# Splitting a weight load and a copy at the start of a fused attention and gated-MLP kernel, and reordering the last additions at its end

## The chip, the cores and the metric

The kernel runs on one core of a Trainium2 chip. The metric is device time in microseconds (us), taken over several executions of the same program. Every execution also leaves the span of the core (first to last instruction), which is about 1.7 us shorter than its time. One execution of each kernel is profiled in full.

All profile lines below are in microseconds from the start of the span unless marked ns. PE is TensorE, PEld its weight loads, DVE is VectorE, ACT is ScalarE, POOL is GpSimd, SP is SyncE; a name with q (SPq, ACTq) is an engine's instruction that issues a DMA.

## The reference, cut to what matters

```python
xn  = layernorm(x)                      # x: 2048 tokens x 512
A   = sliding_window_attention(xn @ wqkv) @ wo      # 32 heads of 16, 8 keys, dilation 2
B   = (z1 * (w_sp @ layernorm(z2) + b_sp)) @ w_out   # z1, z2 = gelu(xn @ w_in), a gated MLP
out = x + A + B
```

Two places matter here. At the start nothing can be multiplied before the first tokens are loaded, normalised and transposed, and before the q weights (a 512 x 512 part of `wqkv`) are there. At the end the last 512 tokens are accumulated in PSUM, `x` is added, and the sum is stored.

## The kernel before: the parts that matter

Tokens are handled in tiles of 128. The first block `t0` has four tiles, each normalised by VectorE, transposed by TensorE into PSUM (`tr`) and copied out by ScalarE (`tr_copy`). TensorE is kept busy at the start by matmuls on a tile of zeros (`warm_up`), which are meant to have its clock full earlier: in this document's profiles it was full by 6.93 us in eleven of the twelve with ten or more of these matmuls (9.82 in the other), and only from 10.21 and 9.50 us in the two with one.

```python
load_x0(SP, 0, 0, 64)           # first token tile, two halves on two queues
load_x0(A, 0, 64, P)
load_x0(A, 1)                   # second token tile
G.dma_start(xall[:, 0, 2:4, :], xblk[0][:, 2:4, :])
load_wqk(SP, 0)                 # q weights, 512 KB
SP.dma_start(xall[:, 1], xblk[1])
load_wqk(SP, 1)                 # k weights, 512 KB
# [cut]
def tr_copy(i, pt):
    A.copy(xnT[:, :, i * P:(i + 1) * P], pt[:])
# [cut]
warm_up(10)
for n in range(2):
    ln_stats(t0[n]); ln_sqrt(col(t0[n]))
for n in range(2):
    ln_tile(t0[n])
    tr_copy(t0[n], tr(t0[n]))
warm_up(1); warm_up(1, 2)
for n in range(2, 4):
    ln_stats(t0[n]); ln_sqrt(col(t0[n]))
for n in range(2, 4):
    ln_tile(t0[n])
pqs = [qk_tile() for _ in range(3)]
qk_part(pqs[0], 0, 0, 0, 2)     # the first q matmuls: eight of 256 columns
tr_copy(t0[2], tr(t0[2]))       # third token tile
```

At the end, the last group's four token tiles (`tb`) lie in PSUM tiles `po` (tb 0 and 1 share one), `pa` (tb 2, and columns 0 to 287 of tb 3) and `pb` (the other 224 columns of tb 3). The order list ends with `Oh3.0 s2.1 Oh3.1 F3.0 F3.1 s3.0 s3.1`: matmuls of tb 0 and 1, matmuls of tb 2 and 3, then `F` (the additions of tb 0 and 1) and `s` (their stores).

```python
def out_half(o, h):
    if o == 3 and h == 1:
        for tb, part, E in ((2, 0, SP), (3, 0, A), (3, 1, SP)):
            out_full(o, tb, part)       # matmuls
            out_add(o, tb, part)        # VectorE: PSUM + x
            out_store(o, tb, part, E)
    else:
        for tb in (2 * h, 2 * h + 1):
            out_full(o, tb)
```

So in VectorE's program the additions of tb 2 and 3 stand before those of tb 0 and 1, although TensorE finishes in the order 0, 1, 2, 3.

## Time and profile before

| | before |
|---|---|
| time, median of the first 3 runs | 206.78 us (206.6 to 207.16) |
| span of the profiled run | 206.2 us |
| first q matmul starts | 8.10 us |
| last matmuls of the last group (po) start | 197.40 us |
| last addition ends | 203.30 us |

The page of the profile, busy time per engine and the chain that ended last (shares of the span):

```profile
PE 199.2 (97%) x1695; PEld 126.2 (61%) x1699; DVE 180.8 (88%) x259; ACT 97.3 (47%) x159; POOL 5.6 (3%) x15
...
PE 94%; DMA 2%; DVE 1%; issue 1%; DVEq 0%; ACTq 0%
```

What TensorE waited for in the whole run (the waits view: total, times, longest):

```profile
PE pwm L547 <- DVE warm L183: 1.1, 1, 1.1
PE pt L221 <- DVE r_x L214: 0.8, 1, 0.8
PE po L520 <- issue: 0.6, 4, 0.2
```

TensorE is the limit from the first q matmul to the end of the last group; a change can gain only before and after that. This is the tail in the timeline (start, duration, engine, line, operation, tiles, count, and in brackets the idle time before it and what ended it):

```profile
199.34 1.85 PE L520 MATMUL pa<-r_w,r_uz 128*128 128x512 bf16 x10
200.62 1.07 DVE L510 TENSOR_TENSOR r_qk<-pa,r_qk 128x512 bf16<-128x512 f32 x2 [6.10 <-PE pa L520]
201.71 0.39 DVE L510 TENSOR_TENSOR r_qk<-pb,r_qk 128x224 bf16<-128x224 f32 x1
202.02 1.28 DVE L510 TENSOR_TENSOR r_qk<-po,r_qk 128x512 bf16<-128x512 f32 x2
```

The additions of `po` come last, at 202.02, though the matmuls that fill `po` had ended before 199.6; VectorE had been idle for 6.10 us before it began with `pa`. And this is the head, the same view:

```profile
1.06 4.45 PE L547 MATMUL pwm<-warm 128*128 128x512 bf16 x10 [1.06 <-DVE warm L183]
6.30 1.13 PE L221 MATMUL pt<-ident,r_x 128*128 128x128 bf16 x8 [0.79 <-DVE r_x L214]
6.94 1.11 ACT L225 COPY xnT<-pt 128x512 bf16<-128x512 bf16 x2 [0.87 <-PE pt L221]
7.22 0.84 PE L547 MATMUL pwm<-warm 128*128 128x512 bf16 x2
8.10 1.86 PE L306 MATMUL pq<-xnT,r_w 128*128 128x256 bf16 x8
```

The two transposed tiles are copied from 6.94 to 8.05, and the first q matmul follows at 8.10. The eight q matmuls take 1.86 us, starting 0.21 to 0.22 us apart, so TensorE still runs at half clock here: in the same trace 32 of them, from 10.84 us on, take 3.49 us by the chain of waits, 0.109 us each.

### The profile page before, as it was taken

Reading aid. Unit: us, or ns where it says so; the run is one execution under the profiler, and the core shown is the slowest. Engines: PE = TensorE matmul, PEld = TensorE weight load, DVE = VectorE, ACT = ScalarE, POOL = GpSimd, SP = SyncE. Lnnn points to the kernel's source line nnn. Section 1 sums busy time; section 2 is a strip of 40 time slices with the busy share of each in tenths; the row PEclk is TensorE's granted clock in tenths of the full one; section 3 lists DMA queues with packets and bytes.
Section 4 is the critical chain, followed back from the end, with each engine's and each line's share of the span. In section 5 each row is a group of like instructions: output and inputs, shape, how many; then the busy total and the mean of one; then the engine's idle time right before and its main releaser. Section 6 shows DMA issues by size and latency. Waiting matters only on the chain.

```text
span 206.2 us, 4083 instructions
## 1 busy us (share of the span) xinstructions
PE 199.2 (97%) x1695; PEld 126.2 (61%) x1699; DVE 180.8 (88%) x259; ACT 97.3 (47%) x159; POOL 5.6 (3%) x15
## 2 busy tenths in 40 slices
PE   7899999999999999999999999999999999999991
PEld 2598866555566666666566666664566654664650
DVE  3979799899679999969999999999999998589604
ACT  3375998879899787634303755430032230020000
POOL 5000000500000000000000000000000000000000
PEclk9999999999999999999999999999999999999998
DMA  5972547400000693199960599998389000465523
GB/s 137 356 257 53 102 101 239 107 0 0 3 0 3 155 182 73 38 234 224 157 168 21 114 199 181 253 206 188 89 152 235 10 3 0 115 147 167 155 97 103
DMA packets 65826, 25.91 MB, mean 126 GB/s; under 512 B 56208, under 2 KB 65488, under 8 KB 65552
## 3 DMA queue, kind: packets, MB, share of 16 engines
q1 hardware_dynamic: 65360, 25.12, 54.9%
q0 software_dynamic: 80, 0.26, 0.5%
q10 hardware_dynamic: 368, 0.27, 0.5%
q8 instruction: 13, 0.21, 0.5%
q14 instruction: 5, 0.04, 0.1%
HBM read 10.13 MB, written 2.10 MB: 59 GB/s over the span
## 4 chain that ended last, share of the span: by engine, by line
PE 94%; DMA 2%; DVE 1%; issue 1%; DVEq 0%; ACTq 0%
PE pg L448 36%; PE pz L235 18%; PE pq L306 14%; PE po L520 7%; PE pv L409 7%; PE po L496 6%; PE pl L359 2%; DMA r_x<-in_A_x_dram 2%; PE pt L221 1%; PE pa L520 1%; PE po L505 1%; PE pb L496 1%; DVE r_qk L510 1%; PE pa L306 0%; DVEq L687 0%
## 5 line engine op out<-in xcount | busy, mean ns | idle before, releaser
L448 PE MATMUL pg<-z,r_qk 128*128 128x344 bf16 x448 | 67.0, 309 | 0.0
L448 PEld LDWEIGHTS <-r_qk 128*128 128x128 bf16 x448 | 43.8, 98 | 21.8
L235 PE MATMUL pz<-w_z,xnT 128*128 128x344 bf16 x256 | 40.3, 309 | 0.0
L423 DVE TENSOR_TENSOR r_pr<-r_x,r_w 128x2048 bf16<-128x2048 bf16 x32 | 38.2, 1218 | 0.4
L454 ACT ACTIVATE gs<-pg,b_col 128x688 bf16<-128x688 f32 x16 | 13.2, 831 | 53.7 <-PE pg L448 53.6
L427 DVE TENSOR_TENSOR r_pr<-r_pr 128x2048 bf16<-128x2048 bf16 x28 | 33.9, 1216 | 0.1
L235 PEld LDWEIGHTS <-xnT 128*128 128x128 bf16 x256 | 24.8, 98 | 13.8 <-issue 1.2
L340 DVE TENSOR_TENSOR r_pr<-r_qk 128x2048 bf16<-128x2048 bf16 x24 | 28.2, 1218 | 2.5 <-ACT r_qk L316 2.5
L306 PE MATMUL pq<-xnT,r_w 128*128 128x256 bf16 (+1 forms) x176 | 29.7, 323 | 0.0
L306 PEld LDWEIGHTS <-r_w 128*128 128x128 bf16 x184 | 20.5, 115 | 7.5 <-issue 0.6
L316 ACT CAST r_qk<-pq 128x1024 bf16<-128x1024 f32 (+1 forms) x16 | 15.4, 993 | 3.7 <-PE pq L306 3.4
L297 ACT ACTIVATE r_uz<-pz 128x688 bf16<-128x688 f32 x16 | 11.6, 744 | 9.7 <-PE pz L235 9.5
L520 PE MATMUL po<-r_w,r_uz 128*128 128x512 bf16 x66 | 14.9, 379 | 0.6 <-issue 0.6
L409 PE MATMUL pv<-xnT,r_w 128*32 128x512 bf16 x256 | 14.6, 380 | 0.0
L496 PE MATMUL po<-r_lg,r_pr 32*128 32x512 bf16 x224 | 14.5, 375 | 0.0
L520 PEld LDWEIGHTS <-r_uz 128*128 128x128 bf16 x85 | 8.0, 98 | 9.8 <-issue 1.5
L351 DVE TENSOR_TENSOR r_pr<-r_pr 128x4096 bf16<-128x4096 bf16 x6 | 13.5, 2285 | 0.0
L203 DVE BATCH_NORM_STATS2 stats<-r_x 128x6 f32<-128x512 bf16 x16 | 10.8, 673 | 2.1 <-DMA r_x<-in_A_x_dram 2.1
L259 ACT ACTIVATE junk<-z 128x688 bf16<-128x688 bf16 x16 | 12.5, 781 | 0.1
L409 PEld LDWEIGHTS <-r_w 128*32 128x32 bf16 x256 | 9.5, 138 | 4.5 <-issue 0.3
L253 ACT ACTIVATE z<-pz 128x688 bf16<-128x688 f32 x16 | 11.8, 741 | 0.5 <-PE pz L235 0.5
L496 PEld LDWEIGHTS <-r_pr 32*128 32x128 bf16 x272 | 7.6, 93 | 6.5 <-issue 0.9
(80 smaller groups left out, 164.0 us busy)
## 6 DMA issues: line engine op xcount, KB each, us to landing
r_lg<-in_A_wo_dram SPq DMA_DIRECT2D x8, 256.0 KB, 4.1
r_qk<-in_A_x_dram SPq DMA_DIRECT2D x16, 128.0 KB, 2.4
out_dram<-r_qk SPq DMA_DIRECT2D x15, 128.0 KB, 2.1
r_w<-in_A_wqkv_dram SPq DMA_DIRECT2D x3, 512.0 KB, 5.6
r_x<-in_A_x_dram SPq DMA_DIRECT2D x3, 512.0 KB, 6.2
w_z<-in_B_w_in_dram SPq DMA_DIRECT2D x2, 688.0 KB, 6.7
r_w<-in_B_w_out_dram SPq DMA_DIRECT2D x1, 640.0 KB, 5.1
r_x<-in_A_x_dram POOLq DMA_DIRECT2D x1, 256.0 KB, 4.3
```

Of the source, the lines that this page charges most:

```text
L235: PE.matmul(pz[:, hh, 0:FHALF], xnT[:, kc, i * P:(i + 1) * P], wz[:, kc, hh * FHALF:(hh + 1) * FHALF], start=(kc == 0), stop=(kc == C - 1))
L306: PE.matmul(pq[:, cc, p0 * P:(p0 + b1 - b0) * P], wqk[:, sd, kc, c0 + cc:D:C], xv[:, kc, b0:b1, j, :], start=(kc == 0), stop=(kc == C - 1))
L316: cast = A.copy(dst, pq[:, :, p0 * P:(p0 + b1 - b0) * P].rearrange("p c (b t) -> p c b t", b=b1 - b0))
L340: prod = V.tensor_tensor(pr[g % 3][:, c].rearrange("p w b t -> p b w t"), q3.unsqueeze(2).broadcast_to([P, TB, 4, P]), k4, ALU.mult)
L351: V.tensor_tensor(pr[g % 3][:, 0:2], pr[g % 3][:, 0:2], pr[g % 3][:, 2:4], ALU.add)
L409: PE.matmul(pv[32 * tb:32 * tb + 32, dd, :], wv[:, kc, 2 * d2 + dd, :], xnT[:, kc, tb * TBS:(tb + 1) * TBS], start=(kc == 0), stop=(kc == ...
L423: V.tensor_tensor(pw_t[n], vp[:, :, off:off + P], a_sb[:, slot_w(w), ts].unsqueeze(1).broadcast_to([P, DH, P]), ALU.mult)
L427: V.tensor_tensor(pw_t[n] if dst is None else dst, pw_t[n], pw_t[m], ALU.add)
L448: PE.matmul(pg[:, hh, 0:FHALF], wsp[n][:, k, :], z2[:, k, hh * FHALF:(hh + 1) * FHALF], start=(k == 0), stop=(k == NT - 1))
L454: A.activation(gs[:], tiles.pop(("g", n))[:, :, 0:FHALF], ACT.Identity, bias=b_col[:, i:i + 1])
L496: PE.matmul(pc, op[32 * tb:32 * tb + 32, d, o * P:(o + 1) * P], wo_r[32 * tb:32 * tb + 32, d, cs], start=(d == 8), stop=False, tile_positi ...
L520: PE.matmul(pc, uT[:, o % 2, m, tb * P:(tb + 1) * P], wout[:, m, cs], start=False, stop=(m == MCH - 3))
```

## The change

Four edits: the q weights come as two halves (rows 0 to 255 and 256 to 511) over the queues of SyncE and ScalarE; the second token tile is copied in two halves, and the first q matmuls are ordered so that those that need only the first half come first; one more warm-up matmul fills the wait before the transposes; and the last group's additions are issued in the order in which TensorE completes them. (The diff also generalises two helpers that give the same program as before; cut here.)

```diff
-Oh3.0 s2.1 Oh3.1 F3.0 F3.1 s3.0 s3.1
+Oh3.0 s2.1 Oh3.1 F3.0 F3.1 s3.0 s3.1 end
# [cut]
-    load_wqk(SP, 0)
+    load_wqk(SP, 0, 0, 2)
+    load_wqk(A, 0, 2, 4)
# [cut]
-    def tr_copy(i, pt):
-        A.copy(xnT[:, :, i * P:(i + 1) * P], pt[:])
+    def tr_copy(i, pt, c0=0, c1=C):
+        A.copy(xnT[:, c0:c1, i * P:(i + 1) * P], pt[:, c0:c1, :])
# [cut: qk_part gets kcs, the row quarters to multiply]
     def out_half(o, h):
-        if o == 3 and h == 1:
-            for tb, part, E in ((2, 0, SP), (3, 0, A), (3, 1, SP)):
+        for tb in (2 * h, 2 * h + 1):
+            for part in range(len(tiles["o", o][tb])):
                 out_full(o, tb, part)
-                out_add(o, tb, part)
-                out_store(o, tb, part, E)
-        else:
-            for tb in (2 * h, 2 * h + 1):
-                out_full(o, tb)
+
+    def last_adds():
+        for tb, part, E in ((2, 0, SP), (3, 0, A), (3, 1, SP)):
+            out_add(3, tb, part)
+            out_store(3, tb, part, E)
# [cut]
-    warm_up(10)
+    warm_up(11)
# [cut]
-        tr_copy(t0[n], tr(t0[n]))
+    tr_copy(t0[0], tr(t0[0]))
+    pt1 = tr(t0[1])
+    tr_copy(t0[1], pt1, 0, 2)
+    tr_copy(t0[1], pt1, 2, 4)
# [cut]
-    qk_part(pqs[0], 0, 0, 0, 2)
+    qk_part(pqs[0], 0, 0, 0, 2, kcs=range(2))
+    qk_part(pqs[0], 0, 0, 0, 2, kcs=range(2, 4))
```

More of the change, by code (lines that the diff above doesn't have):

```diff
@@ L40 @@
 ORD = [1, 2, 3, 0]
-PAIRED = (0, 1, 2, 3, 4, 5, 6, 7)
+CHUNKS = (2, 2, 2, 2, 2, 2, 2, 2)
 ORDER = """
@@ L165, in load_x0, with load_wqk @@
         E.dma_start(xall[p0:p1, 0, tb, :], x2[tb * TBS + p0:tb * TBS + p1, :])
-    def load_wqk(E, s):
-        E.dma_start(wqk[:, s],
-                    A_wqkv[:, s * D:(s + 1) * D].rearrange("(k p) f -> p k f", p=P))
+    def load_wqk(E, s, k0=0, k1=C):
+        E.dma_start(wqk[:, s, k0:k1],
+                    A_wqkv[:, s * D:(s + 1) * D].rearrange("(k p) f -> p k f", p=P)[:, k0:k1])
     load_x0(SP, 0, 0, 64)
@@ L298, in z1_gelu, with qk_part @@
                      tiles.pop(("x", n))[:, :, 0:FHALF], ACT.Gelu_apprx_tanh)
-    def qk_part(pq, j, m, b0, b1, ccs=(0, 1), p0=None):
+    def qk_part(pq, j, m, b0, b1, ccs=(0, 1), p0=None, kcs=range(C)):
         sd, c0 = m // 2, 2 * (m % 2)
@@ L304, in qk_part @@
         for cc in ccs:
-            for kc in range(C):
+            for kc in kcs:
                 PE.matmul(pq[:, cc, p0 * P:(p0 + b1 - b0) * P], wqk[:, sd, kc, c0 + cc:D:C],
@@ L348, in pair_add, with pair_add2 @@
     def pair_add(g):
-        if g not in PAIRED:
-            return
         V.tensor_tensor(pr[g % 3][:, 0:2], pr[g % 3][:, 0:2], pr[g % 3][:, 2:4], ALU.add)
+    def pair_add2(g):
+        V.tensor_tensor(pr[g % 3][:, 0], pr[g % 3][:, 0], pr[g % 3][:, 1], ALU.add)
     def logits(g):
@@ L355, in logits @@
         pl = ps_aux.tile([P, 4, P], F32, name="pl", tag="aux")
-        n_c = 2 if g in PAIRED else C
+        n_c = CHUNKS[g]
         for c in range(n_c):
@@ L650 @@
     st = z2_var(3, 3) + [z2_log, z2_exp]
-    steps = {"z": z2_mm, "zg": z2_gelu, "zs": z2_sq, "q": qk_mm, "qc": qk_cast, "p": prod_c, "a": pair_add,
+    steps = {"z": z2_mm, "zg": z2_gelu, "zs": z2_sq, "q": qk_mm, "qc": qk_cast, "p": prod_c, "a": pair_add, "b": pair_add2,
              "L": logits, "Lc": logits_cast, "V": v_mm, "Vc": v_cast, "X": z1_mm, "Xg": z1_gelu,
@@ L656 @@
              "G": g_mm, "Gi": g_bias, "U": u_mul, "T": u_tr, "A": lambda k: ap[k](),
-             "O": out_heads, "Or": out_rest, "Oh": out_half, "F": out_add, "s": out_store,
+             "O": out_heads, "Or": out_rest, "Oh": out_half, "F": out_add, "s": out_store, "end": last_adds,
              "halo": halo_zero, "wo": load_wo, "late": load_late, "xr": load_xr, "w": load_wsp}
```

## The prediction

> **What bounds the kernel.** TensorE: the page gives PE 97% of the 206.2 us span, the chain of waits is 94% PE. Between 8.1 and 197 us TensorE waits for nothing (the waits view has only four 0.2 us "issue" pauses). The change moves work only in the head (before 8.1 us) and the tail (after 201.2), so it can win only there, and what it wins at the head should come through nearly whole.
>
> **Tail.** The timeline shows the additions of po (token tiles 0 and 1 of the last group) placed last on VectorE, at 202.02 to 203.30, although TensorE ended their matmuls at about 198.6 and 199.5 and VectorE sat idle 6.1 us until 200.62. Their second 128 KB store is issued at 203.3, and the span ends 2.9 us later. The change runs these additions first, in the idle time (0.68 us each), so the last work is the small pb addition, which ended at 202.10: 1.2 us off the chain. The last store is then 56 KB instead of 128 KB (landing 1.5 against 2.1 us in the list of DMA issues), perhaps 0.2 us more. If both additions wait for the shared po tile until 199.5, the others slip by up to 0.25 us. Tail: -1.3 us (-1.0 to -1.6).
>
> **Head.** The first q matmul started at 8.10. Its weights were there (load issued at 1.47, 5.6 us to landing). It waited for the copy of the second token tile (7.46 to 8.05); the warm-up matmuls ahead would have let it go at about 7.86. So splitting the weight load buys nothing by itself. A half copy should take about 0.38 us (estimate: part of the 0.59 is fixed), so four matmuls can start near 7.86: -0.24 us. Against it, three copies hold ScalarE about 0.15 us longer before the square root of tile 2 (7.94), and a third DMA issue (0.6 us) precedes its table load (2.04; needed at 4.54): no harm.
>
> **Clock.** Matmuls of 256 columns are 0.213 us apart until about 10 us, 0.109 after. [...] The trace agrees that it doubles; whether the phase varies no run here shows yet. [...] Then up to 1 us of half-speed work goes away, but VectorE's normalisation of tiles 2 and 3 (ending 8.88 and 9.40) bounds TensorE, and the half copy gains nothing. Over both cases: head -0.25 us (0 to -1.0).
>
> **Prediction.** 206.78 - 1.3 - 0.25 = 205.2 us; 8 in 10: 204.5 to 205.9. Faster by over 2%: 0.02; within: 0.97; slower: 0.01.
>
> **What would show it.** Tail: po's additions before pa's, starting by 199.6; the span ends about 5.4 us after po's last matmul rather than 6.7. Head: the first q matmul within 0.5 us of the transposes; the time at which spacing falls to 0.109 us tells the clock's phase.
>
> **What would make it wrong.** An end that doesn't follow the last addition (a fixed drain); the second half of the weights landing late on ScalarE's queue; x tile 1 (landed at 4.81, on the chain) pushed back by new traffic; the clock's phase differing between runs by more than the gain.

The sum came to 205.2 us (206.78 - 1.3 - 0.25). The second of the "both cases" behind the head's -0.25 (0 to -1.0), an earlier full clock (from "Then" on), rests on an assumption. The clock's phase means, here and in the expectations, the time at which the clock becomes full: 3.74 to 10.21 us in the profiles below.

## The result

Ratios are the mean time of one kernel's runs over that of the other's in the same rounds, so they are not quite the ratio of the medians quoted beside them.

| | before | changed |
|---|---|---|
| median | 206.69 us | 205.20 us |
| range (4 runs each) | 206.44 to 207.16 | 205.09 to 205.32 |
| ratio, 95% interval | | 0.9925 (0.9906 to 0.9945) |
| span of the profiled run | 206.2 us | 203.6 us |

The gain is 1.49 us, 0.7%, at 205.20 us: the predicted time to the last digit given. But the two profiled spans differ by 2.6 us, not by 1.5. So the pair of profiles can't be read naively; the execution of the kernel before that was profiled took 207.95 us, longer than any of its timed runs of these rounds. The page after:

```profile
PE 197.8 (97%) x1696; PEld 125.3 (62%) x1700; DVE 180.5 (89%) x259; ACT 97.5 (48%) x160; POOL 5.4 (3%) x15
...
PE 92%; DMA 4%; DVE 1%; SPq 1%; issue 1%; DVEq 0%
```

The tail after, in the timeline:

```profile
198.28 1.85 PE L522 MATMUL pa<-r_w,r_uz 128*128 128x512 bf16 x10
198.48 1.29 DVE L512 TENSOR_TENSOR r_qk<-po,r_qk 128x512 bf16<-128x512 f32 x2 [5.02 <-PE po L522]
199.68 1.05 DVE L512 TENSOR_TENSOR r_qk<-pa,r_qk 128x512 bf16<-128x512 f32 x2
200.65 0.39 DVE L512 TENSOR_TENSOR r_qk<-pb,r_qk 128x224 bf16<-128x224 f32 x1
```

`po` now comes first, and the last addition is the small one of `pb`. Measured from the start of po's last matmuls (197.40 before, 196.33 after, by the chain of waits), the last addition ends 5.90 us later before (203.30) and 4.71 us later after (200.65 + 0.39 = 201.04): 1.19 us less. From there to the end of the span it is 2.86 us before and 2.56 us after. Together the tail is 1.5 us shorter in this pair.

The head after:

```profile
1.06 4.12 PE L549 MATMUL pwm<-warm 128*128 128x512 bf16 x11 [1.06 <-DVE warm L184]
5.78 0.92 PE L222 MATMUL pt<-ident,r_x 128*128 128x128 bf16 x8 [0.61 <-DVE r_x L215]
6.22 1.17 ACT L226 COPY xnT<-pt 128x512 bf16<-128x512 bf16 x3 [0.66 <-PE pt L222]
7.16 1.08 PE L307 MATMUL pq<-xnT,r_w 128*128 128x256 bf16 x8
8.41 0.40 PE L222 MATMUL pt<-ident,r_x 128*128 128x128 bf16 x4 [0.17 <-DVE r_x L215]
```

Three things differ. The eight q matmuls take 1.08 us, not 1.86: the clock was already full. The clock record of the trace says so too: full clock begins at 9.82 us in the profile before and at 4.28 us in this one. The spacing of the matmuls agrees: in the profile before, the third tile's transposes start 94 ns apart at 9.76 and 55 or 56 ns apart from 9.85 on. The first transposes begin 0.52 us earlier (5.78 against 6.30), because the second token tile landed earlier (its statistics began at 4.35 instead of 4.83). And TensorE now waits for VectorE before the third tile's transposes at 8.41. A new wait also shows in the view of waits: the weight load at 10.02 waited for the k weights to land (total, times, longest):

```profile
PEld L307 <- DMA r_w<-in_A_wqkv_dram: 0.4, 1, 0.4
```

From these two profiles alone, about 1.1 us (197.40 to 196.33) seem to be won at the head. Whether the head edits won them, or chance did, is the question for the experiments.

**Theory A:** nearly the whole gain is the tail; the two profiles differ at the head because of the clock's phase and of when the x tiles happened to land. **Rival B:** the head edits win about 1 us. **Rival C:** the half copy and the split load win something by themselves, besides the clock.

### The profile page after: what moved, and what is told of

Same layout as the page of the kernel before. It is cut to its first block, busy times and chain, and to the rows that moved or that the text cites. A ratio compares the mean times of both kernels' runs of the same rounds, so it can differ in the third digit from the quotient of the medians.

```text
span 203.6 us, 4089 instructions
## 1 busy us (share of the span) xinstructions
PE 197.8 (97%) x1696; PEld 125.3 (62%) x1700; DVE 180.5 (89%) x259; ACT 97.5 (48%) x160; POOL 5.4 (3%) x15
## 4 chain that ended last, share of the span: by engine, by line
PE 92%; DMA 4%; DVE 1%; SPq 1%; issue 1%; DVEq 0%
PE pg L450 37%; PE pz L236 18%; PE pq L307 12%; PE po L522 7%; PE pv L411 7%; PE po L498 6%; DMA r_w<-in_A_wqkv_dram 4%; PE pl L361 2%; DVE r_qk L512 1%; PE po L507 1%; PE pb L498 1%; PE pa L307 0%; SPq L168 0%; SPq L165 0%; SPq L177 0%
## 5 line engine op out<-in xcount | busy, mean ns | idle before, releaser
L307 PE MATMUL pq<-xnT,r_w 128*128 128x256 bf16 (+1 forms) x176 | 29.1, 316 | 0.2
L512 DVE TENSOR_TENSOR r_qk<-po,r_qk 128x512 bf16<-128x512 f32 x14 | 9.1, 682 | 6.4 <-PE po L522 6.4
```

The source lines that it names most:

```text
L307: PE.matmul(pq[:, cc, p0 * P:(p0 + b1 - b0) * P], wqk[:, sd, kc, c0 + cc:D:C], xv[:, kc, b0:b1, j, :], start=(kc == 0), stop=(kc == C - 1))
```

## The experiments

Times of runs that share rounds have the same runs of the kernel before beside them: 206.67 us (206.47 to 207.81) for runs 1 to 4, 207.24 us (206.6 to 208.98) for 5 to 8 on another chip, 206.82 us (206.42 to 208.45) for 9 to 12.

### Run 1: the tail alone

The kernel before, with the new `out_half`, `last_adds` and `end` and nothing else of the diff.

> Before plus the reordered last additions only. Theory A (nearly the whole gain is the tail): -1.3 us, -1.0 to -1.6 against before in the same rounds, and the span ends 7.2 to 7.4 us after the start of po's last matmuls (8.8 in before). Rival B (what the pair of profiles suggests, where the first po matmul moved from 197.40 to 196.33: most is won at the head): at most -0.6 us. The clock's phase may still differ from run to run.

Measured: 205.43 us (205.36 to 205.63, 5 runs), ratio 0.9934 (0.9915 to 0.9954). That is -1.24 us between the medians. From the start of po's last matmuls (196.56) the span took 7.35 us more (203.91), against 8.76 us in the first profile before. The tail edit alone gives most of the change's 1.49 us; rival B's -0.6 us falls. The tail in its timeline is that of the changed kernel, and the last addition again ends 4.71 us after the start of po's matmuls:

```profile
198.71 1.29 DVE L510 TENSOR_TENSOR r_qk<-po,r_qk 128x512 bf16<-128x512 f32 x2 [5.02 <-PE po L520]
199.91 1.04 DVE L510 TENSOR_TENSOR r_qk<-pa,r_qk 128x512 bf16<-128x512 f32 x2
200.88 0.39 DVE L510 TENSOR_TENSOR r_qk<-pb,r_qk 128x224 bf16<-128x224 f32 x1
```

Its head is the old one, and yet its view of waits shows the wait for the k weights too (they landed at 10.20; the other of the two waits is for the q weights at 7.25, and no matmul was held up by it):

```profile
PEld L306 <- DMA r_w<-in_A_wqkv_dram: 1.1, 2, 0.5
```

So this wait is not a product of the new head.

### Run 2: the head alone

The kernel before, with the other edits and the old tail.

> Before plus the three head edits (eleventh warm-up, split q load, half copy), old tail. Theory A: 0 to -0.4 us in the median, with less spread between runs than before has; the k weights landing near 10.0 us are the floor of the head. Rival B: -0.9 to -1.1 us.

Measured: 206.88 us (206.35 to 207.48, 6 runs), ratio 1.0004 (0.998 to 1.0027). The head edits alone move nothing that these runs can see. The expected smaller spread did not come: three runs lay at 206.35 to 206.68, three at 207.08 to 207.48. Rival B falls a second time.

### Run 3: the eleventh warm-up matmul alone

```diff
-    warm_up(10)
+    warm_up(11)
```

> Before plus the eleventh warm-up matmul alone. Theory A: the clock's phase is the only real difference between the heads of the two profiles, so this gives the same as the whole head edit within 0.2 us: 0 to -0.4 us. Rival C (the half copy and split load make the head's gain): 0.0, and head_only is 0.25 us or more below it.

Measured: 206.88 us (206.52 to 207.58, 6 runs), ratio 1.0008 (0.9985 to 1.0031), the same median as the whole head. So rival C does not show in the times either, and the one warm-up matmul wins nothing in the median.

### Run 4: the changed kernel with ten warm-up matmuls

```diff
-    warm_up(11)
+    warm_up(10)
```

> The changed kernel with ten warm-up matmuls again. Theory A: median within 0.3 us of the changed kernel (205.2), perhaps with single runs up to 1 us longer when the clock doubles near 10 us instead of before 7. Rival B or C: the same as the changed kernel in every run (205.1 to 205.3).

Measured: 205.35 us (205.19 to 206.55, 6 runs), ratio 0.9938 (0.9911 to 0.9965). Five runs lay at 205.19 to 205.46, one at 206.55. That is what theory A expected, but a single late run proves nothing of its cause, for it was not the profiled one.

### Run 5: the kernel before, once more

No edit; a control, and a second draw of the profile.

> The kernel before, unchanged, once more, as a control and for a second profile. If the clock of TensorE doubles before about 7 us in this profile (it doubled near 10.1 us in the first), theory A expects po's last matmuls to start at 196.1 to 196.6 us, as in the profiles of the changed kernel, not at 197.4, and the time to be the median 206.6 to 206.8. Ratio of the timed runs 1.000 within 0.003. Rival B (the head edits are worth 1 us): po's last matmuls start near 197.4 again.

Measured: 206.64 us (206.35 to 207.61, 6 runs), ratio 0.9971 (0.9934 to 1.0008). The profiled execution took 206.56 us, and its clock was full from 5.08 us on. Its head in the timeline:

```profile
5.84 0.92 PE L221 MATMUL pt<-ident,r_x 128*128 128x128 bf16 x8 [0.48 <-DVE r_x L214]
6.27 1.11 ACT L225 COPY xnT<-pt 128x512 bf16<-128x512 bf16 x2 [0.66 <-PE pt L221]
7.43 1.04 PE L306 MATMUL pq<-xnT,r_w 128*128 128x256 bf16 x8 [0.35 <-ACT xnT L225]
8.47 0.40 PE L221 MATMUL pt<-ident,r_x 128*128 128x128 bf16 x4
```

This is the kernel before, and po's last matmuls start at 196.09 us in it, earlier than the changed kernel's 196.33. So the pair of first profiles had compared a late draw of one kernel with an early draw of the other. With this profile the tail can be compared at the same clock:

```profile
199.31 1.07 DVE L510 TENSOR_TENSOR r_qk<-pa,r_qk 128x512 bf16<-128x512 f32 x2 [6.10 <-PE pa L520]
200.40 0.39 DVE L510 TENSOR_TENSOR r_qk<-pb,r_qk 128x224 bf16<-128x224 f32 x1
200.71 1.28 DVE L510 TENSOR_TENSOR r_qk<-po,r_qk 128x512 bf16<-128x512 f32 x2
```

The last addition ends at 201.99, again 5.90 us after the start of po's matmuls, and the span at 204.80, 8.71 us after it. The changed kernel takes 7.27 us for the same stretch (196.33 to 203.60), and 7.28 us in its second profile (run 11). By these two profiles the tail edit is worth 1.44 us. Over all profiles the stretch is 8.63 to 8.78 us with the old tail (five) and 7.27 to 7.35 us with the new one (eight, run 7 left out), so 1.3 to 1.5 us.

### Run 6: k weights before the second x block

```diff
-    SP.dma_start(xall[:, 1], xblk[1])
     load_wqk(SP, 1)
+    SP.dma_start(xall[:, 1], xblk[1])
```

> The changed kernel with the k weights' load issued before that of the second x block on SyncE's queue. Theory A (in the head of the changed kernel TensorE ends up waiting for the k weights, which landed near 10.0 us, for 0.37 us): the k weights land near 8.5 us, the wait goes away, and the time falls by 0.2 to 0.4 us to 204.8 to 205.0. Rival: the second x block, now landing near 10 us instead of 8.5, holds up VectorE by over 1 us and TensorE later: 205.2 or more.

Measured: 205.47 us (205.21 to 206.11, 6 runs), ratio 0.9914 (0.9879 to 0.995). No gain, and no clear loss. The k weights landed at 8.36, as expected, and its profile has no wait for weights. Run 11, the control without this edit, has none either: there the k weights landed 6.8 us after their issue at 2.83, at about 9.6, while in the first profile of the changed kernel they took 7.1 us and landed at about 10. So the wait comes and goes with the landing, and curing it does not show in the median. There was no control of the changed kernel on this chip, so a gain of 0.1 us isn't excluded.

### Run 7: the last token tile stored whole

```diff
# [shortened: statements joined in a line, the line that sets i cut, comment added]
-        for tb, part, E in ((2, 0, SP), (3, 0, A), (3, 1, SP)):
-            out_add(3, tb, part)
-            out_store(3, tb, part, E)
+        out_add(3, 2); out_store(3, 2)
+        out_add(3, 3, 0); out_add(3, 3, 1)
+        SP.dma_start(out2[i * P:(i + 1) * P, :], ot_t[3])    # 128 KB in one piece
```

> The changed kernel with the last token tile stored in one piece of 128 KB after its second addition instead of 72 and 56 KB. If the smaller last store is worth about 0.2 us, as predicted: +0.1 to +0.5 us (205.3 to 205.7). If only the time of the last addition counts: 205.2, unchanged.

Measured: 205.58 us (205.34 to 205.84, 6 runs), ratio 0.9914 (0.988 to 0.9948), 0.11 us above run 6 of the same rounds, which is within the spread of either. The profile shows it more sharply:

```profile
200.51 0.39 DVE L512 TENSOR_TENSOR r_qk<-pb,r_qk 128x224 bf16<-128x224 f32 x1
200.93 0.33 SPq L536 DMA_DIRECT2D out_dram<-r_qk  x1
```

The last addition ends at 200.90 and the span at 203.71, 2.81 us later: as in the kernel before (2.81 in run 5, 2.86 in the first profile) and 0.25 us more than in the changed kernel (2.56). So the tail's 1.44 us are 1.19 us of order and 0.25 us of a smaller last store. The 1.19 us repeat within 0.01 us in every profile; the 0.25 us are less sure, for this last stretch is 2.73 to 2.88 us in the five profiles with the old tail and 2.56 to 2.65 us in the eight with the new one (0.1 to 0.3 us).

This run also bears on the clock. The trace's clock record begins, with full clock, at 6.44 us:

```profile
1.06 4.88 PE L552 MATMUL pwm<-warm 128*128 128x512 bf16 x11 [1.06 <-DVE warm L184]
5.91 0.92 PE L222 MATMUL pt<-ident,r_x 128*128 128x128 bf16 x8
7.47 1.03 PE L307 MATMUL pq<-xnT,r_w 128*128 128x256 bf16 x8 [0.31 <-ACT xnT L226]
```

In the first profile before, ten warm-up matmuls had ended at 5.51, the transposes began at 6.30, and the clock was full only from 9.82. Here eleven ended at 5.94, the transposes began at 5.91, and it was full from 6.44. But two things differ, the eleventh matmul and the earlier transposes (the second x tile had landed earlier), and no run separates them. And with ten matmuls the clock was full from 5.08 in run 5 and from 3.78 in run 4. So that the eleventh matmul raises the clock earlier is not shown.

### Run 8: the head alone, again

> The head edits alone once more (the runs of the first time fell in two groups, 206.35 to 206.68 and 207.08 to 207.48). If the groups are chance (clock phase or landing of loads), about a third to a half of these runs are again over 207; the fast group within 0.1 us of before's fast group (206.5), so that the head edits are worth under 0.2 us. Rival B: all under 206.

Measured: 206.46 us (206.4 to 206.78, 6 runs), ratio 0.9961 (0.9923 to 0.9999). No run was over 207 this time, so the two groups of run 2 are not a property of the kernel. The ratio below 1 comes from the many long runs of the kernel before in these rounds (five of 11 over 207.6). Its shortest run is 206.4; the kernel before has 206.35 (run 5) and 206.6 on this chip. Its head in the timeline, at full clock as in run 5's profile:

```profile
5.74 0.92 PE L222 MATMUL pt<-ident,r_x 128*128 128x128 bf16 x8 [0.83 <-DVE r_x L215]
7.12 1.03 PE L307 MATMUL pq<-xnT,r_w 128*128 128x256 bf16 x8
8.38 0.40 PE L222 MATMUL pt<-ident,r_x 128*128 128x128 bf16 x4 [0.22 <-DVE r_x L215]
```

### Runs 9 and 10: one warm-up matmul only, new and old head

Both with the new tail. In run 9 the changed kernel's `warm_up(11)` becomes `warm_up(1)`; in run 10 the kernel of run 1 gets the same.

> The changed kernel with one warm-up matmul at the start instead of eleven[...]. Theory A (the clock's late doubling near 10 us is what makes slow runs): 206.2 to 206.8, about 1.0 to 1.5 us above the changed kernel in the same rounds, with the clock doubling at 9.5 us or later in the profile. If the clock did not matter: unchanged, 205.2 to 205.5.

> The same with the old head (whole copy, one q load) and the new tail, one warm-up matmul. The half copy was predicted to win 0.24 us while the clock is low: 0.15 to 0.3 us above the cold kernel with the new head. If the half copy wins nothing in either state: equal to it within 0.1 us.

Measured: run 9 206.97 us (206.02 to 208.67), ratio 0.9998 (0.9949 to 1.0046); run 10 207.04 us (205.87 to 208.96), ratio 1.0005 (0.9952 to 1.0058). Without the warm-up the median of run 9 is 1.7 us above the control of run 11, a little more than the 1.0 to 1.5 us expected, and each run differs from the next, over 2.65 us and more. The clock was full from 10.21 and 9.50 us in the two profiles. The times are too spread to tell 0.2 us between the two heads. The profiles can, for the first steps, measured from the first transposes. First run 9 (new head), then run 10 (old head):

```profile
5.98 1.13 PE L222 MATMUL pt<-ident,r_x 128*128 128x128 bf16 x8 [4.31 <-DVE r_x L215]
7.57 1.89 PE L307 MATMUL pq<-xnT,r_w 128*128 128x256 bf16 x8
9.24 0.63 PE L222 MATMUL pt<-ident,r_x 128*128 128x128 bf16 x4
```

```profile
5.74 1.13 PE L221 MATMUL pt<-ident,r_x 128*128 128x128 bf16 x8 [4.08 <-DVE r_x L214]
7.54 1.87 PE L306 MATMUL pq<-xnT,r_w 128*128 128x256 bf16 x8
9.20 0.53 PE L221 MATMUL pt<-ident,r_x 128*128 128x128 bf16 x4
```

At half clock the new head starts the q matmuls 1.59 us after the first transposes instead of 1.80, and the third tile's transposes 3.26 us after instead of 3.46. So the half copy is worth 0.2 us here up to the third tile's transposes. That it lasts is not shown: po's last matmuls start at 197.56 and 197.17, which is 191.58 us after the first transposes with the new head and 191.43 with the old one. The clock can account for that, for it rose 4.23 us after the first transposes in run 9 and 3.76 us in run 10.

### Run 11: the changed kernel, again

> The changed kernel unchanged, as the control of these rounds on this chip: 205.1 to 205.4, ratio to before 0.992 to 0.995 (on a chip where before has many slow runs, lower).

Measured: 205.25 us (205.09 to 205.72, 6 runs), ratio 0.9911 (0.9874 to 0.9947). The same time as in the first rounds; against the median before of these rounds, -1.57 us.

### Run 12: a twelfth warm-up matmul

> The changed kernel with a twelfth warm-up matmul. [...]fewer slow runs than the control, median the same. If the twelfth matmul (0.43 us at half clock) runs into the transposes: up to +0.1 us, and no fewer slow runs.

Measured: 205.43 us (205.11 to 206.04, 6 runs), ratio 0.9916 (0.9882 to 0.995). Not better than eleven. In its profile the clock was full only from 6.80 us, the twelve matmuls ran until 6.36, and the first transposes stood at 6.16, 1.88 us after the second tile's statistics began (4.28), where all the other profiles have 1.43 to 1.47 us. The twelfth matmul had run into them.

### What the profiles say together

| profile | head | full clock from | second tile's statistics | first transposes | first q matmul | third tile's transposes | po's last matmuls | po minus first transposes |
|---|---|---|---|---|---|---|---|---|
| before | old | 9.82 | 4.83 | 6.30 | 8.10 | 9.76 | 197.40 | 191.10 |
| run 5, before again | old | 5.08 | 4.41 | 5.84 | 7.43 | 8.47 | 196.09 | 190.25 |
| run 3, one more warm-up | old | 4.09 | 4.43 | 5.90 | 7.49 | 8.53 | 196.14 | 190.24 |
| run 8, head alone | new | 3.74 | 4.31 | 5.74 | 7.12 | 8.38 | 195.99 | 190.25 |
| run 11, changed | new | about 4.30 (by matmul spacing, none on record) | 4.44 | 5.87 | 7.25 | 8.50 | 196.12 | 190.25 |
| changed | new | 4.28 | 4.35 | 5.78 | 7.16 | 8.41 | 196.33 | 190.55 |

At full clock the new head starts the first q matmul 1.38 us after the first transposes, the old one 1.59 us. But the third tile's transposes follow 2.63 or 2.64 us after the first ones in all five of these: the new head has TensorE wait there for VectorE (the bracket in the changed kernel's line at 8.41), where the old one arrives just in time. From the first transposes to po's last matmuls it is 190.25 us within 0.01 with either head; the changed kernel's first profile loses 0.30 to the wait for the k weights. Of the profiles that the table leaves out, runs 4 and 2 (new head, clock full by 3.94) have 190.24 and 190.29; run 1 (old head) has 190.70, for it waited longest for the k weights; runs 7, 12 and 6, where the clock rose only after the first transposes (6.44 to 6.93), have 190.29, 190.31 and 190.43. So at full clock the half copy and the split load are worth nothing that these profiles show, and the start of the first transposes, which follows the landing of the second x tile, decides. The late clock goes with 0.85 us in the first profile before (191.10 against 190.25), the late tile with another 0.46 us (6.30 against 5.84); together that is the 1.31 us between the two profiles of one and the same kernel. The 0.85 us alone are more than half of this change's 1.49 us, and over all the profiles the clock became full anywhere from 3.74 us (run 8) to 10.21 us (run 9).

What stays open: why some runs are longer. In the five sets of its timed runs together, the kernel before had 10 runs of 43 above 207.25 us, the changed kernel none of 10 more than 0.63 us above its shortest. But with eleven warm-up matmuls and the old tail (runs 2, 3 and 8) there were 4 of 18 above 207.25. A late clock and a late tile account for one long run, the first profiled one; none of the other long runs was profiled, so how much the eleventh matmul cuts their number is not settled. The tail may have a part in it: with the old tail and ten or more warm-up matmuls 14 of 61 runs lay more than 0.9 us above the shortest, with the new tail 3 of 39, and none of run 1's five, which have the old head and ten warm-up matmuls. No run tests this.

## Why the prediction was right or wrong

The time was right, 205.2 us predicted and 205.20 us measured. One term of its sum was too small and the other too large.

- **TensorE bounds the kernel, only the two ends can gain.** Right. Po's last matmuls start 190.24 to 190.29 us after the first transposes with either head, where the clock was full by then and no weights were late.
- **"1.2 us off the chain" from the order of the additions.** Right: the last addition ends 1.19 us earlier relative to po's matmuls, in the pair of profiles and against run 5.
- **The smaller last store, "perhaps 0.2 us more".** Right: 0.25 us by run 7, 0.1 to 0.3 over all profiles.
- **"Tail: -1.3 us (-1.0 to -1.6)".** The mechanism is right, the term a little too small: it measured -1.44 us in the profiles at the same clock (1.3 to 1.5 over all profiles), and -1.24 us in the medians of run 1. The span ended 5.15 us after po's last matmul (198.45), against 6.65 before; 5.4 was expected.
- **"If both additions wait for the shared po tile until 199.5, the others slip by up to 0.25 us".** They do wait: the first addition starts at 198.48, only when both tiles' matmuls had ended (196.33 + 2.12). Nothing slipped at the end: pb's addition starts 4.32 us after the start of po's matmuls, 4.31 before.
- **"Splitting the weight load buys nothing by itself".** Right as far as the runs go. In the five profiles with the whole load it landed 5.0 to 5.7 us after 1.47, by 7.2, and no first q matmul waited for it. The first half landed 4.5 to 5.1 us after 1.47, hardly sooner than the whole, though it is half the size, and the second half by 6.6 to 7.6, no sooner than the whole.
- **The half copy: "0.38 us", "four matmuls can start near 7.86: -0.24 us".** Right at half clock for the steps that follow: the half copy took 372 ns (the whole one 586), the q matmuls came 0.21 us earlier and the third tile's transposes 0.20 us (runs 9 and 10); whether the gain lasts to the end is not shown. Right at full clock too: the prediction said that then the half copy gains nothing, and the table shows it.
- **No harm from a third DMA issue on ScalarE.** Right: the table load began at 2.52 instead of 2.04, and the square root it serves at 4.47, where VectorE's statistics, not the table, held it.
- **"Over both cases: head -0.25 us (0 to -1.0)".** This is the term that was mis-sized. It averaged over early and late clock as if late were usual, as in the profile it had. In the profiles the early clock is usual (full by 6.93 in eleven of the twelve with ten or more warm-up matmuls), so the median run of the kernel before had nothing to win: runs 2, 3 and 8 gave ratios of 1.0004, 1.0008 and 0.9961, the last with an interval to 0.9999 and against rounds with many long runs. The head is worth about 0 in the median.
- **"Landing late on ScalarE's queue" and "pushed back by new traffic", among what could make it wrong.** The second showed in no run. Of the first there is a trace without effect: in the changed kernel's first profile the second half landed at 7.57, after the first q matmuls had begun (7.16), and the eight took 1.08 us, not the 1.03 of runs 2, 8 and 11; the wait at 8.41 swallowed that. The wait that did cost time was another: for the k weights, with a longest wait of 0.4 us in the changed kernel and 0.5 in run 1, which the prediction did not consider. In those two profiles, with an early clock, TensorE reaches the third tile's transposes, ahead of the k weights, at 8.41 and 8.49 us, against 9.76 with the late clock.
- **"The clock's phase differing between runs by more than the gain".** Named as a risk, and true of the profiles: it made the pair of spans show 2.6 us for a gain of 1.5.

The errors of -0.25 in the head and +0.14 in the tail (1.44 against 1.3) nearly cancel, so the agreement to the last digit is partly luck.

## What to carry to other kernels

When TensorE is busy throughout, look at what follows its last matmul: put the work that is ready first, first in each engine's program (1.19 us here), and let the last store be small (56 KB instead of 128 KB: 0.25 us here by run 7, 0.1 to 0.3 over the profiles). Before a step at the start is made faster, see whether the step that follows waits for another engine: here, at full clock, the first q matmul came 0.21 us sooner after the first transposes (1.38 us instead of 1.59), and the third tile's transposes no sooner (2.63 or 2.64 us in both). Measure from a common event (here the first transposes) to a late one, not from the start of the span. Before two profiles are compared, check that each is a typical run by its own time, and take a second profile of the same kernel if it isn't.
